# Turning ten of eighteen normalised tiles by DMA through DRAM instead of on TensorE

## The chip, the cores and the metric

The kernel runs on one core of a Trainium2 chip. The metric is the device time of one execution in microseconds (us), from the first to the last instruction with what lies around it. Below, PE is TensorE (PEld its weight loads), DVE is VectorE, ACT is ScalarE, POOL is GpSimd and SP is SyncE, whose queue issues every DMA of this kernel.

## What is computed

Sliding-window attention, cut here to what matters, then a feed-forward block with a softmax-weighted activation and a LayerNorm (FFN 1), then a gated feed-forward block (FFN 2), all in float32:

```python
scores = where(mask, scale * q @ k.T + bias, -1e9)      # 4 x 8 heads, 576 tokens, window 128
x = (softmax(scores) @ v)                               # 2304 tokens x 512

h = x @ w_in                                            # 2304 x 1024
solu = h * softmax(h)
ln = (solu - mean(solu)) / sqrt(var(solu) + 1e-6) * g_ln
y = ln @ w_out                                          # 2304 x 512

g = y @ w_gate                                          # 2304 x 1536
out = (g * sigmoid(g) * (y @ w_val)) @ w_out2           # 2304 x 512
```

## The kernel before

The 2304 tokens are 18 tiles of 128. The attention runs in 20 steps (4 batches of 5 query tiles) of four units of two heads. A unit's scores (line 441) are exponentiated (480), scaled by the inverse of the row sum (491 to 493, mostly on POOL), turned by PE with an identity matrix (511, "the probabilities' turns") and multiplied with v and with the difference vd of two v tiles (553). vd is made by POOL (403) from two loaded v tiles, of which three are kept.

FFN 1 takes a tile through three coroutines. `up(i)` multiplies x by w_in (24 products, line 639, "U" below), takes maximum, exponential, sums and variance (662 to 690), and normalises e, a tile of 128 tokens x 1024 features, in place on DVE or POOL (698). `flip(i)` turns e so that features lie on partitions: eight 128x128 transposes on PE into two PSUM banks (719), then ACT rounds the bank to the high part lnT0 (255), and DVE subtracts to get the low part lnT1 (259). Every product with FFN weights is made of three products of such high and low parts. `down1(i)` multiplies lnT by w_out (24 products, line 639, "the down product"), separates the result into its 16-bit halves (751) and stores these to DRAM (yscr), from where FFN 2 reads them back with six transposing DMAs (918).

FFN 2 follows when the attention is over: its first weights (dw<-w) are loaded then, and its products (968, 1130) fill the rest of the program.

The order of the work is made when the program is built. Coroutines hand operations to an `Emitter`, a list scheduler with a price for each operation and a rank for each coroutine (`i + LEAD` and offsets such as `O_FLIP`). It takes the operation that can start first by its prices, then the lowest rank. An operation with several possible engines (`high`, `low`) goes to the one that would end first, with a handicap `B_DVE` or `B_ACT` for DVE and ACT. `PATIENCE` says how long tiled products of the attention may be held back in favour of full-size ones. At run time each engine, and SP's DMA queue too, works through its list strictly in order and waits on semaphores. Four e tiles (`E1`) and two lnT pairs exist.

Of the kernel before, what the change touches and what calls it, by code (L numbers as in the profile page):

```python
# [11 lines left out]
U16 = mybir.dt.uint16  # L12
# [6 lines left out]
B, H, S, D = 4, 8, 576, 64  # L19
# [4 lines left out]
P = 128  # L24
NPAIR = H // 2
NQT = 5
NTT = NT // P
# [13 lines left out]
PXB = 2  # L41
EB = 5
Q = 32
PTB = 4
WHOLE = 20
VDB = 3
# [1 line left out]
LEAD = 3.373  # L48
R_FLIP = 0.751
R_DOWN = 3.0  # L50
PW_IN = [-0.63, -0.23, -0.29, -0.28, 0.25, 0.26, 0.43, 0.28]
PW_OUT = 5.23
B_DVE = 1802.444
B_ACT = 700.0
HALVES = [(0, 1), (1, 0), (0, 0)]
HB = NC2 // 2
# [10 lines left out]
O_FLIP = -1.299  # L67
O_LN = -0.416
O_SET = 0.102
O_FREE = -1.226  # L70


TOGETHER = 100000.0
PATIENCE = 540.469
LEAST = 3
BIAS = {"DVE": B_DVE, "ACT": B_ACT}

# [148 lines left out]
def attention_then_two_ffns(ctx: ExitStack, tc: tile.TileContext, qk, v, w_in, w_out, g_ln, w2, ident_d, base_d, tri_d, out):  # L226


    nc = tc.nc
    em = Emitter()  # L230
    PE, DVE, ACT, POOL, DMA = "PE", "DVE", "ACT", "POOL+", "DMA"
    DVEP, NONE = "DVE+", "POOL"
    yscr = nc.dram_tensor("yscr", [NT, 2, DM], U16).ap()
    ascr = nc.dram_tensor("ascr", [P, NC2, NT], F32).ap()
    wscr = nc.dram_tensor("wscr", [P, HB, 7 * 256], F32).ap()

    def t_act(n, sbuf=True, table=False):
        return (94 if sbuf else 51) + 94 * table + 0.833 * n

    def t_dve(n, fast=False):  # L240
        return 68 + (0.52 if fast else 1.042) * n

    def t_pool(n):
        return 149 + 2.104 * n

    def dma(dst, src, nbytes, deps=()):
        return (DMA, max(445.0, nbytes / 345.0), lambda: nc.sync.dma_start(dst, src), deps, 2000.0)

    const = ctx.enter_context(tc.tile_pool(name="const", bufs=1))
    ident = const.tile([P, P], F32, name="ident")  # L250
# [3 lines left out]
    def high(hi, src, n, sbuf=True):  # L254
        return [(ACT, t_act(n, sbuf), lambda: nc.scalar.copy(hi, src)),  # L255
                (DVEP if sbuf else DVE, t_dve(n, sbuf), lambda: nc.vector.tensor_copy(hi, src))]

    def low(lo, src, hi, n, sbuf=True):
        ways = [(DVEP if sbuf else DVE, t_dve(n), lambda: nc.vector.tensor_sub(lo, src, hi.bitcast(F32)))]  # L259
        if sbuf:  # L260
            ways.append((POOL, t_pool(n), lambda: nc.gpsimd.tensor_sub(lo, src, hi.bitcast(F32))))
        return ways
# [60 lines left out]
    at = esa.enter_context(tc.tile_pool(name="at", bufs=1, side="right"))  # L323
# [84 lines left out]

    e_s, pt_s, st_s, px_s = Slots(EB), Slots(PTB), Slots(EB), Slots(PXB)
    px_of, pts = {}, {}  # L410
# [4 lines left out]
    def score(c, qd):  # L415
# [19 lines left out]
        def scores():  # L435
            for j in range(2):
                for i in range(0, n, Q):
                    o, k0, w = (j * 256, 0, P) if t == 0 else (j * 256 + i, (t - 1) * P + i, P + Q)
                    for r in range(2):
                        rows = slice(r * D, (r + 1) * D)  # L440
                        nc.tensor.matmul(banks[ks[r]][i:i + Q, o:o + w], raw[c][rows, 2 * qd + j, i:i + Q],  # L441
                                         kt[rows, 2 * qd + j, k0:k0 + w], start=True, stop=True)
# [12 lines left out]
    def attend(u):  # L455
# [50 lines left out]
        tp = banks[k][:, 0:2 * P].rearrange("p (j q) -> p j q", j=2)  # L506
        pt = at.tile([P, 2, 2, P], F32, tag="pt", bufs=PTB, name="pt")

# [93 lines left out]
    def load_in():  # L602
        for half in range(2):
            cs = slice(half * 512, half * 512 + 512)
            for r in range(KM):
                def one(half=half, r=r, cs=cs):
                    yield from decode(win[0][:, r, cs], win[1][:, r, cs], w_in[r * P:(r + 1) * P, cs])
                d = em.start(one(), PW_IN[half * KM + r])
                chain(d, win_ok[half][r])
# [16 lines left out]

    lnT, es = {}, {}
    h_s, e1_s, ln_s, ys_s = Slots(HU), Slots(E1), Slots(2), Slots(1)
    upped = [Done() for _ in range(NTT)]
    normed = [Done() for _ in range(NTT)]  # L630
    flipped = [[Done(), Done()] for _ in range(NTT)]
# [72 lines left out]

    def flip(i):
        yield normed[i]
        if i:
            yield flipped[i - 1][1]
        yield ln_s
        lnT[i] = [m1.tile([P, KF1, P], F32R, tag=f"lnT{a}", bufs=2, name=f"lnT{a}") for a in range(2)]  # L710
        e = es[i]
        tail_ = []
        for q in range(2):
            bk = yield bank_s
            tp = banks[bk].rearrange("p (k c) -> p k c", k=4)

            def turn(q=q, tp=tp):
                for k in range(4):
                    nc.tensor.transpose(tp[:, k], e[:, q, k * P:(k + 1) * P], ident)

            hi, lo = (y[:, 4 * q:4 * q + 4] for y in lnT[i])
            x = yield (PE, 436, turn, (), 0.0, O_FLIP)
            y = yield (high(hi, tp, 512, False), [x], 0.0, O_LN)
            y = yield (low(lo, tp, hi, 512, False), [y], 0.0, O_LN)
            em.give(bank_s, y, bk)
            tail_.append(y)
        em.give(e1_s, x)
        for q, y in enumerate(tail_):
            yield y
            flipped[i][q].settle(y.time)  # L730
# [452 lines left out]
    for bank in banks:  # L1183
        halves = bank.rearrange("p (j c) -> p j c", j=2)
        nc.vector.memset(halves[:, :, P + Q:2 * P], 0.0)
        nc.vector.memset(halves[:, :, 0:P - Q], 0.0)
    for c in range(NS):
# [55 lines left out]
```

## Time and profile before

| | us |
|---|---|
| median of 3 runs | 755.77 |
| lowest, highest | 754.22, 757.95 |
| the profiled execution | 753.33 |
| its span | 751.5 |
| PE busy in the span | 717.4 (95%) |
| DVE, ACT, POOL busy | 554.5, 458.2, 225.4 |

The span runs from the first to the last instruction of the core; 1.83 us of the execution lie around it. Busy times count what an engine executes; instructions on PE overlap, so their durations don't add up to time. Idle time of an engine costs nothing by itself unless the engine sets the pace. Rows of the profile are in a section of their own below. A row of instructions in time gives start, length, engine, line, operation, output and inputs with their shapes and count, and in brackets the idle time of the engine ahead of it and what ended that.

### The profile page before, as it was taken

The page shows a single profiled execution, that of the slowest core. Times are in us where ns is not written, and L with a number is a line of the kernel's source. Part 1 is how long each engine was busy: PE and PEld are TensorE (multiplying, and loading weights), DVE is VectorE, ACT ScalarE, POOL GpSimd, SP SyncE. Part 2 cuts the span into 40 slices and gives each one's busy share as a digit, 9 for nine tenths or more (in the row PEclk, how much of TensorE's full clock was granted, in tenths as well). Part 3 has the DMA queues.
Part 4 walks back from the last instruction along what each step waited for, and adds up shares of the span by engine and source line. Part 5 has one row for each costly group of instructions (what it writes and reads, how often), then busy time and mean ns, then how long its engine had stood idle before and what let it go on. Part 6 is the DMA issues. An engine that isn't in the chain of part 4 may idle for free. (4 is left out here: it accounts for less than half of the span.)

```text
span 751.5 us, 14447 instructions
## 1 busy us (share of the span) xinstructions
PE 717.4 (95%) x5164; PEld 637.3 (85%) x5164; DVE 554.5 (74%) x1522; ACT 458.2 (61%) x1129; POOL 225.4 (30%) x240
## 2 busy tenths in 40 slices
PE   3879989999999999999999999999999999999997
PEld 1547667778788887888899999999899999999997
DVE  4788985676657665989879766876664599887965
ACT  7899996666656665687466555655553575442531
POOL 3686673333332422550024331221310000220200
PEclk9999999999999999999999999999999999999999
DMA  8753221222221006153755545554341698786951
GB/s 267 220 190 107 85 73 49 92 72 64 72 65 29 22 15 157 54 155 94 179 186 159 185 137 175 176 167 157 119 147 64 240 351 289 255 290 210 304 161 64
DMA packets 68328, 110.84 MB, mean 147 GB/s; under 512 B 24992, under 2 KB 37664, under 8 KB 68256
## 3 DMA queue, kind: packets, MB, share of 16 engines
q1 hardware_dynamic: 68256, 109.93, 44.9%
q8 instruction: 40, 0.66, 0.3%
q14 instruction: 32, 0.26, 0.1%
HBM read 76.09 MB, written 29.10 MB: 140 GB/s over the span
## 5 line engine op out<-in xcount | busy, mean ns | idle before, releaser
L968 PE MATMUL bank<-yt,w 128*128 128x384 f32 x1008 | 183.3, 337 | 2.6 <-ACT t L989 1.6
L968 PEld LDWEIGHTS bank<-yt,w 128*128 128x128 f32 x1008 | 175.5, 188 | 5.6 <-ACT set L989 2.6
L1130 PE MATMUL bank<-w,wo 128*128 128x384 f32 x756 | 132.8, 336 | 0.0
L1130 PEld LDWEIGHTS bank<-w,wo 128*128 128x128 f32 x756 | 132.4, 188 | 0.0
L301 POOL TENSOR_TENSOR db<-db,dw 128x512 int32<-128x512 int32 x52 | 72.1, 1387 | 187.6 <-DVE db L299 140.1
L639 PE MATMUL bank<-wout,lnT 128*128 128x512 f32 x432 | 102.8, 392 | 0.1
L968 PE MATMUL bank<-shared,w 128*128 128x384 f32 x504 | 96.5, 340 | 2.2 <-ACT set L991 1.4
L639 PEld LDWEIGHTS bank<-wout,lnT 128*128 128x128 f32 x432 | 80.3, 188 | 17.5 <-issue 0.8
L968 PEld LDWEIGHTS bank<-shared,w 128*128 128x128 f32 x504 | 87.3, 188 | 7.0 <-ACT set L989 2.3
L480 ACT ACTIVATE e<-e,st 128x128 f32<-128x128 f32 (+1 forms) x160 | 62.6, 402 | 35.8 <-DVE st L475 33.6
L639 PE MATMUL bank<-shared,shared 128*128 128x512 f32 x288 | 81.9, 416 | 1.1 <-ACT shared L255 1.1
L493 POOL TENSOR_TENSOR e<-e,st 128x256 f32<-128x256 f32 (+1 forms) x68 | 42.1, 622 | 77.7 <-DVE st L486 68.2
L639 PEld LDWEIGHTS bank<-shared,shared 128*128 128x128 f32 x288 | 52.3, 194 | 13.4 <-issue 2.0
L255 ACT CAST w<-t 128x768 fp32r<-128x768 f32 (+2 forms) x33 | 26.4, 809 | 42.2 <-DVE t L1084 29.5
L293 ACT ACTIVATE dw<-dw 128x512 int32<-128x512 uint32 x52 | 35.2, 676 | 14.0 <-DMA dw<-w 9.9
L475 DVE CUSTOM_DVE_ANT_0 e<-bank,bias 128x128 f32<-128x128 f32 (+1 forms) x160 | 38.3, 282 | 4.6 <-PE bank L441 2.4
L994 DVE TENSOR_TENSOR set<-set,bank 128x384 f32<-128x384 f32 x34 | 18.8, 553 | 30.4 <-PE bank L968 23.3
L441 PE MATMUL bank<-keys,raw 64*32 64x160 f32 (+1 forms) x1152 | 31.8, 322 | 9.7 <-DMA keys<-qk 7.7
L511 PE MATMUL bank<-ident,e 128*128 128x128 f32 (+1 forms) x160 | 29.8, 291 | 10.8 <-POOL e L493 4.3
L639 PE MATMUL bank<-shared 128*128 128x512 f32 x144 | 38.9, 391 | 0.0
L511 PEld LDWEIGHTS bank<-ident,e 128*128 128x128 f32 (+1 forms) x160 | 18.7, 146 | 23.5 <-POOL e L493 7.9
L255 ACT CAST w<-db 128x512 fp32r<-128x512 f32 (+1 forms) x47 | 26.8, 570 | 19.0 <-POOL db L301 14.5
(106 smaller groups left out, 1221.7 us busy)
## 6 DMA issues: line engine op xcount, KB each, us to landing
dw<-w SPq DMA_DIRECT2D x36, 512.0 KB, 3.9
t<-ascr SPq DMA_DIRECT2D x21, 768.0 KB, 5.7
ascr<-set SPq DMA_DIRECT2D x34, 384.0 KB, 2.7
later<-ascr SPq DMA_DIRECT2D x15, 768.0 KB, 5.5
wo<-wscr SPq DMA_DIRECT2D x6, 896.0 KB, 7.4
raw<-qk SPq DMA_DIRECT2D x19, 256.0 KB, 2.9
yscr<-ys SPq DMA_DIRECT2D x18, 256.0 KB, 2.0
wscr<-db SPq DMA_DIRECT2D x18, 256.0 KB, 4.3
```

Of the source, the lines that this page charges most:

```text
L255: return [(ACT, t_act(n, sbuf), lambda: nc.scalar.copy(hi, src)), (DVEP if sbuf else DVE, t_dve(n, sbuf), lambda: nc.vector.tensor_copy(hi ...
L293: r = yield (ACT, t_act(512), lambda: nc.scalar.activation(a, lw, AF.Copy, scale=2.0 ** -29), (), 0.0, O_DEC)
L301: x = yield (POOL, t_pool(512), lambda: nc.gpsimd.tensor_tensor(b.bitcast(I32), b.bitcast(I32), a, ALU.add), [x, r], 0.0, O_DEC)
L441: nc.tensor.matmul(banks[ks[r]][i:i + Q, o:o + w], raw[c][rows, 2 * qd + j, i:i + Q], kt[rows, 2 * qd + j, k0:k0 + w], start=True, stop=True)
L475: d = yield (DVE, t_dve(P), lambda j=j: nc.vector.tensor_tensor_reduce(e[0:n, j], sc[0:n, j * 256:j * 256 + P], bias[0:n, 2 * pr + j, bs], ...
L480: ex.append((yield (ACT, 93 + t_act(P, True, True), lambda j=j: nc.scalar.activation(e[0:n, j], e[0:n, j], AF.Exp, bias=st[0:n, j:j + 1], ...
L493: eng.tensor_tensor(e[0:n], e[0:n], st[0:n, 6:8].unsqueeze(2).to_broadcast([n, 2, P]), ALU.mult)
L511: nc.tensor.transpose(tp[:, j, 0:n], e[0:n, j], ident[0:n, 0:n])
L639: nc.tensor.matmul(o, terms[m][0], terms[m][1], start=(m == 0), stop=(m == len(terms) - 1))
L968: nc.tensor.matmul(o, l, r, start=first and m == 0, stop=m == 5, skip_group_check=True)
L994: g2 = yield (DVE, t_dve(NH), lambda: nc.vector.tensor_add(t[:, 1], t[:, 1], sb), [x3, u2], 0.0, O_FREE)
L1130: nc.tensor.matmul(o, w[:, b], ob[k, i][a][:, j], start=i == 0 and m == 0, stop=i == HB - 1 and m == 2)
```

## The change

For tiles 4 to 13 `flip(i)` no longer uses PE. Each half q of e (512 features) is copied into a tile pl with the two 16-bit halves of each word in two planes (on ACT, DVE or POOL; `halves_of`). pl is stored to DRAM (lscr, 256 KB), and a transposing DMA reads it back into the same half of e, now with features on partitions. The high and low parts of lnT are then made from e in SBUF, the high part by ACT or DVE, the low part by DVE or POOL. e is given back only after that. Two pl tiles exist. The other eight tiles are turned by PE as before. Four numbers of the scheduler change as well. (escr is declared and not used.)

```diff
+FLIP_BY_DMA = range(4, 14)
+PLB = 2
...
-PW_IN = [-0.63, -0.23, -0.29, -0.28, 0.25, 0.26, 0.43, 0.28]
+PW_IN = [-0.63, -0.23, -0.29, -0.28, 0.25, 0.17, 0.43, 0.28]
-B_DVE = 1802.444
+B_DVE = 1863.684
...
-O_FREE = -1.226
-TOGETHER = 100000.0
-PATIENCE = 540.469
+O_FREE = -1.17
+TOGETHER = 96722.643
+PATIENCE = 36.086
...
+    lscr = nc.dram_tensor("lscr", [NTT, 2, P, 2, 512], U16).ap()
...
+    def turn_by_dma(dst, src, nbytes, deps=()):
+        return (DMA, max(445.0, nbytes / 250.0), lambda: nc.sync.dma_start_transpose(dst, src), deps, 2200.0)
+
+    def halves_of(dst, src, n):
+        words = src.bitcast(U16).rearrange("p (c h) -> p h c", h=2)
+        return [(ACT, t_act(2 * n), lambda: nc.scalar.copy(dst, words)),
+                (DVEP, t_dve(2 * n), lambda: nc.vector.tensor_copy(dst, words)),
+                (POOL, t_pool(2 * n), lambda: nc.gpsimd.tensor_copy(dst, words))]
...
     def flip(i):
         yield normed[i]
+        e = es[i]
+        if i in FLIP_BY_DMA:
+            r = e.rearrange("p q (k t) -> p q k t", k=4)
+            words = r.rearrange("p q k t -> p q (k t)").bitcast(U16).rearrange("p q (k t) -> p q k t", k=4)
+            back = []
+            for q in range(2):
+                yield pl_s
+                pl = at.tile([P, 2, 512], U16, tag="pl", bufs=PLB, name="pl")
+                x = yield (halves_of(pl, e[:, q], 512), (), 0.0, O_FLIP)
+                x = yield dma(lscr[i, q], pl, 262144, [x])
+                em.give(pl_s, x)
+                x = yield turn_by_dma(words[:, q], lscr[i, q].rearrange("t h c -> (t h) c"), 262144, [x])
+                back.append(x)
+            yield back[0]
         if i:
             yield flipped[i - 1][1]
         yield ln_s
         lnT[i] = [m1.tile([P, KF1, P], F32R, tag=f"lnT{a}", bufs=2, name=f"lnT{a}") for a in range(2)]
-        e = es[i]
+        if i in FLIP_BY_DMA:
+            ends = []
+            for q in range(2):
+                hi, lo = (y[:, 4 * q:4 * q + 4] for y in lnT[i])
+                y = yield (high(hi, r[:, q], 512), [back[q]], 0.0, O_LN)
+                y = yield (low(lo, r[:, q], hi, 512), [y], 0.0, O_LN)
+                ends.append(y)
...
+            em.give(e1_s, y)
+            return
```

New lines are numbered higher than old ones: products of FFN 1 stand at 653 (639), the probabilities' turns at 524 (511), the turns of normalised tiles at 758 (719), loads and stores at 251 (247).

Since the scheduler sets the order, the change moves instructions well beyond the turns. The first place is PE around the first down product. Before, with bank_84 the up product of a half tile, wout and lnT_915 the first down product, e the probabilities, and e_1015 the normalised tile 2:

```order
L639 MATMUL bank_84<-shared_74,shared_73 128x512 x4
L639 MATMUL bank_84<-shared_73,shared_74 128x512 x4
L639 MATMUL bank_84<-shared_73 128x512 x4
L639 MATMUL bank_80<-wout_76,lnT_915 128x512 x8
L639 MATMUL bank_80<-wout_75,lnT_916 128x512 x8
L639 MATMUL bank_80<-wout_75,lnT_915 128x512 x8
L511 MATMUL bank_83<-ident,e 128x128 x2
L719 MATMUL bank_86<-ident,e_1015 128x128 x4
```

The same place on PE in the changed kernel:

```order
L653 MATMUL bank_84<-shared_74,shared_73 128x512 x4
L653 MATMUL bank_84<-shared_73,shared_74 128x512 x2
L524 MATMUL bank_85<-ident,e 128x128 x2
L653 MATMUL bank_83<-wout_76,lnT_915 128x512 x8
L653 MATMUL bank_83<-wout_75,lnT_916 128x512 x8
L653 MATMUL bank_83<-wout_75,lnT_915 128x512 x8
L524 MATMUL bank_81<-ident,e 128x128 x2
L524 MATMUL bank_82<-ident,e 128x128 x2
L653 MATMUL bank_84<-shared_73,shared_74 128x512 x2
L653 MATMUL bank_84<-shared_73 128x512 x4
```

Six of the twelve up products moved behind the first down product, and a pair of the probabilities' turns moved ahead of it.

The second place is POOL ahead of that down product: the last two rows of w_out (wout1), e1 a normalised tile, e the probabilities, mst the statistics of a tile. Before:

```order
L261 TENSOR_TENSOR wout1_76<-db_1298,wout0_75 128x512
L695 TENSOR_TENSOR mst_1150<-mst_1150,mhalf_59 128x1
L261 TENSOR_TENSOR wout1_76<-db_1365,wout0_75 128x512
L698 TENSOR_SCALAR e1_1278<-e1_1278,mst_1150 128x512 x2
L493 TENSOR_TENSOR e_1438<-e_1438,st_1439 128x256
```

Now:

```order
L274 TENSOR_TENSOR wout1_76<-db_1298,wout0_75 128x512
L709 TENSOR_TENSOR mst_1150<-mst_1150,mhalf_59 128x1
L506 TENSOR_TENSOR e_1436<-e_1436,st_1437 128x256
L274 TENSOR_TENSOR wout1_76<-db_1365,wout0_75 128x512
L712 TENSOR_SCALAR e1_1278<-e1_1278,mst_1150 128x512 x2
L506 TENSOR_TENSOR e_1522<-e_1522,st_1523 128x256
L260 COPY pl_1579<-e1_1278 128x1024
```

A scaling of probabilities (e_1436, which ACT did before) stands ahead of the last row of w_out, and the first separation into 16-bit planes follows.

The third place is POOL in the second half of the attention. Before, with e1_2451 the normalised tile 8, e1_2640 tile 9, and e the probabilities:

```order
L698 TENSOR_SCALAR e1_2451<-e1_2451,mst_2213 128x512 x2
L493 TENSOR_TENSOR e_2556<-e_2556,st_2557 64x256
L493 TENSOR_TENSOR e_2558<-e_2558,st_2559 64x256
L493 TENSOR_TENSOR e_2568<-e_2568,st_2569 64x256
L493 TENSOR_TENSOR e_2570<-e_2570,st_2571 64x256
L695 TENSOR_TENSOR mst_2450<-mst_2450,mhalf_59 128x1
L698 TENSOR_SCALAR e1_2640<-e1_2640,mst_2450 128x512 x2
```

Now, with e1_2444 tile 8 and e1_2634 tile 9:

```order
L712 TENSOR_SCALAR e1_2444<-e1_2444,mst_2190 128x512 x2
L260 COPY pl_2568<-e1_2444 128x1024
L506 TENSOR_TENSOR e_2562<-e_2562,st_2563 64x256
L506 TENSOR_TENSOR e_2564<-e_2564,st_2565 64x256
L506 TENSOR_TENSOR e_2577<-e_2577,st_2578 64x256
L506 TENSOR_TENSOR e_2579<-e_2579,st_2580 64x256
L709 TENSOR_TENSOR mst_2443<-mst_2443,mhalf_59 128x1
L274 TENSOR_TENSOR lnT1_2685<-e1_2444,lnT0_2684 128x512 x2
L712 TENSOR_SCALAR e1_2634<-e1_2634,mst_2443 128x512 x2
L260 COPY pl_2775<-e1_2634 128x1024
```

Tile 8's separation and, once it is back from DRAM, its two subtractions stand between the scalings of probabilities, and the subtractions stand ahead of tile 9's normalisation. SP's queue there has two stores and two transposing reads per tile among the attention's loads. On the whole PE has 80 turns fewer, DVE 20 subtractions to lnT1 fewer; POOL has 20 such subtractions and 8 separations more, ACT 12 separations more, and SP 40 DMAs more.

## Rows read from the trace of the kernel before

**Rows 1.** Busy time by stretch: us, then PE, PEld, DVE, ACT, POOL, clock, DMA.
```profile
110.00:340.00 230.00, 229.25 (x1908) 184.99 (x1908) 159.47 (x610) 150.49 (x448) 85.85 (x110) 1.00 0.24 73
340.00:560.00 220.00, 215.22 (x1200) 207.53 (x1199) 168.84 (x313) 129.05 (x255) 53.38 (x45) 1.00 0.50 159
...
140.00:280.00 140.00, 139.40 (x1392) 112.00 (x1391) 95.30 (x428) 89.58 (x302) 50.43 (x71) 1.00 0.17 52
```

**Rows 2.** PE in time, at the turns of tiles 6, 10 and 13.
```profile
171.15 1.04 PE L719 MATMUL bank<-ident,e 128*128 128x128 f32 x8
172.02 0.82 PE L511 MATMUL bank<-ident,e 128*128 128x128 f32 x6
...
234.62 1.36 PE L719 MATMUL bank<-ident,e 128*128 128x128 f32 x8
235.82 0.82 PE L511 MATMUL bank<-ident,e 128*128 128x128 f32 x6
...
283.68 1.09 PE L719 MATMUL bank<-ident,e 128*128 128x128 f32 x8
284.71 0.58 PE L511 MATMUL bank<-ident,e 64*128 64x64 f32 x6
```

**Rows 3.** PE's weight loads in time, at changes of form.
```profile
167.05 0.20 PEld L553 LDWEIGHTS bank<-pt,vd 128*64 128x64 f32 x4 [0.35 <-issue]
...
168.08 2.59 PEld L639 LDWEIGHTS bank<-wout,lnT 128*128 128x128 f32 x12 [0.17 <-issue]
```

**Rows 4.** Groups of instructions: count, busy us, mean ns, idle; the last from 140 to 280 us.
```profile
L259 DVE TENSOR_TENSOR lnT<-bank,lnT 128x512 fp32r<-128x512 f32 x36 | 23.9, 684 | 8.4 <-ACT lnT L255 8.2
L751 ACT COPY ys<-bank 128x1024 uint16<-128x1024 uint16 x18 | 18.1, 1005 | 8.1 <-PE bank L639 7.3 <-ACT w L255 0.9
L261 POOL TENSOR_TENSOR shared<-db,shared 128x512 fp32r<-128x512 f32 x8 | 10.1, 1272 | 2.4 <-ACT shared L255 2.4
...
L698 POOL TENSOR_SCALAR e<-e,mst 128x512 f32<-128x512 f32 x16 | 12.2, 776 | 0.8
```

**Rows 5.** PE and POOL in time, at the first down product.
```profile
109.72 2.11 PE L639 MATMUL bank<-shared,shared 128*128 128x512 f32 x8
110.98 1.30 POOL L261 TENSOR_TENSOR wout<-db,wout 128x512 fp32r<-128x512 f32 x1 [0.40 <-ACT wout L255]
112.57 5.61 PE L639 MATMUL bank<-wout,lnT 128*128 128x512 f32 x24
```

**Rows 6.** POOL and PE in time: tile 9's normalisation, turns and down product.
```profile
204.54 1.53 POOL L698 TENSOR_SCALAR e<-e,mst 128x512 f32<-128x512 f32 x2
...
212.97 0.62 POOL L493 TENSOR_TENSOR e<-e,st 128x256 f32<-128x256 f32 x1 [0.24 <-DVE st L486]
...
219.27 1.04 PE L719 MATMUL bank<-ident,e 128*128 128x128 f32 x8
...
245.51 5.61 PE L639 MATMUL bank<-wout,lnT 128*128 128x512 f32 x24
```

**Rows 7.** DMA issues (count, KB, median us to landing); line 918 on SP's queue (ns).
```profile
t<-ascr SPq DMA_DIRECT2D x21, 768.0 KB, 5.7
yscr<-ys SPq DMA_DIRECT2D x18, 256.0 KB, 2.0
...
L918 SPq DMA_TRANSPOSE t<-yscr x6: 3054/3274/4268, 287.7 to 358.8; - x6
DMA to landing us min/median/max: 5.2/5.8/7.8
```

**Rows 8.** POOL and DVE in time, at FFN 2's inputs.
```profile
299.68 3.00 POOL L698 TENSOR_SCALAR e<-e,mst 128x512 f32<-128x512 f32 x2
...
300.50 0.95 DVE L259 TENSOR_TENSOR yt<-t,yt 128x768 fp32r<-128x768 f32 x1
```

**Rows 9.** POOL and PE in time, from v's difference to the first product with it.
```profile
214.06 2.54 POOL L403 TENSOR_TENSOR vd<-v 128x512 f32<-128x512 f32 x2 [0.47 <-DMA v<-v]
...
237.95 0.44 PE L553 MATMUL bank<-pt,vd 128*64 128x128 f32 x4
```

More of the change, by code (lines that the diff above doesn't have):

```diff
@@ L233, in attention_then_two_ffns @@
     yscr = nc.dram_tensor("yscr", [NT, 2, DM], U16).ap()
+    escr = nc.dram_tensor("escr", [H // 2 * B * NQT, P, 2, 2 * P], U16).ap()
+    lscr = nc.dram_tensor("lscr", [NTT, 2, P, 2, 512], U16).ap()
     ascr = nc.dram_tensor("ascr", [P, NC2, NT], F32).ap()
@@ L628, in attention_then_two_ffns @@
     h_s, e1_s, ln_s, ys_s = Slots(HU), Slots(E1), Slots(2), Slots(1)
+    pl_s = Slots(PLB)
     upped = [Done() for _ in range(NTT)]
@@ L710, in flip @@
         lnT[i] = [m1.tile([P, KF1, P], F32R, tag=f"lnT{a}", bufs=2, name=f"lnT{a}") for a in range(2)]
-        e = es[i]
+        if i in FLIP_BY_DMA:
[5 more added lines that the diff above has]
+                ends.append(y)
+            for q, y in enumerate(ends):
+                yield y
+                flipped[i][q].settle(y.time)
+            em.give(e1_s, y)
+            return
         tail_ = []
```

## The prediction

> **What bounds the kernel now.** I read the table of stretches first [rows 1], then PE's own order in time [rows 2, 5, 6]. In the stretch from 110 to 340 us, where the attention steps, both products of FFN 1 and the turns share PE, PE is busy for 229.25 of 230 us at a granted clock of 1.00; between 140 and 280 us it is busy for 139.40 of 140, while DVE has 95.30, ACT 89.58 and POOL 50.43. PE thus idles 0.75 us in 230. So in the stretch that the change touches the bound is PE's own sequence: an instruction that leaves PE shortens the program by what it held there, as long as nothing else comes to end later than PE.
>
> **What the change takes from PE.** Each of the ten tiles loses eight 128x128 turns. They overlap, so what counts is start to start and not how long one lasts. Tile 6 starts its eight at 171.15, and the next instruction starts at 172.02: 0.87 us. Tile 13, whose next turns are 64 wide, has 283.68 to 284.71: 1.03 us. Of the ten tiles six are like the first (0.87 to 0.88), three like the second (1.02 to 1.03), and tile 10 has 234.62 to 235.82, 1.20 us, which I count at 0.87, because the rest looks like a wait inside it [rows 2]. Sum: 7 x 0.87 + 3 x 1.03 = 9.2 us. Bounds: 10 x 0.87 = 8.7, and 6 x 0.87 + 3 x 1.03 + 1.20 = 9.5.
>
> On PE one turn of a row thus takes 0.87 / 8 = 0.109 us [rows 2]. The Trainium skill's page "VectorE: DVE Perf Modes", section The three transpose paths, gives 390 ns for a 128x128 transpose on TensorE and 1309 ns by DMA, and its rules say TensorE where PSUM will do; by its figure for TensorE the ten tiles would save 80 x 0.39 = 31 us, an estimate that the trace contradicts.
>
> **What it adds on the path: a gap at the first down product.** PE is also re-ordered. Before, twelve products of an up stage (the U that starts at 109.72) stand ahead of the first down product, which starts at 112.57, right when POOL has finished the last row of w_out (110.98 + 1.30 = 112.28) [rows 5]. Now only six products and one pair of turns stand there, and POOL has one more scaling of probabilities ahead of that last row. In the old trace POOL idles 0.40 us in this place [rows 5]; such a scaling takes 0.62 [rows 6], so w_out would be there some 0.2 us later, at about 112.5. The down product starts when it did, but less is done by then: six products are half of 109.72 to 112.57, about 1.4 us, and a pair of turns gives back 0.2 (two of 0.109). I take 1.3 us, with what the scaling adds; ends 0 (if w_out comes earlier in the new order) and 2.0 (if the scaled probabilities come later too).
>
> **Changes of PE's form.** Between full-size products and the tiled ones of the attention PE's weight loads idle 0.17 to 0.35 us [rows 3]. The new order has 115 runs of one form on PE, the old one 112: 3 x 0.26 = 0.8 us; ends 0 and 1.1.
>
> **What it adds beside the path.** Per tile, by the nearest rows [rows 4]:
> - Two separations into 16-bit planes (1024 elements). Twelve of twenty stand on ACT, where the copy of ys, the same size and type from PSUM, takes 1.005 us. Eight stand on POOL, where no such copy is shown; a one-input operation of half the size takes 0.776 us, a two-input one 1.272, so 1.6 to 2.5; I take 1.6, since a copy has one input. Per tile on average: 1.2 on ACT, 0.8 x 1.6 = 1.3 on POOL.
> - The two roundings to hi stay on ACT. The two subtractions to lo move from DVE (684 ns each) to POOL (1.272 each): DVE -1.4, POOL +2.5.
> - Two stores of 256 KB and two transposing reads. A store of this size lands in 2.0 us. The six transposes in the trace are three times as large: 3.27 us of SP's queue each, and 5.8 to landing [rows 7]. No engine waits for SP itself; what is queued behind on it are loads of v, raw and k, which are asked for well ahead (the difference of two v tiles made at 214.06 serves a product at 237.95 [rows 9]). By size the new ones hold SP for 1.1 us; as long as the old ones is the other end.
>
> A tile comes every 16.1 us (171.15 to 283.68 is seven tiles [rows 2]). Of these ACT works 89.58 / 140 x 16.1 = 10.3, then 11.5; DVE 11.0, then 9.6; POOL 5.8, then 9.6; the new cadence would be about 15.2. No engine comes near PE. The length of the way doesn't show either: tile 9 is normalised at 204.54 + 1.53 = 206.07, turned by PE from 219.27 on, and first used by its down product at 245.51 [rows 6]. The new way (separation 1.0 to 2.5, store 2.0, two issues 2.2, landing at most 5.8, two subtractions 2.5) takes 13.5 to 15 us, inside the 39; even the old instant of the turn is missed by no more than 2 us, so the four e tiles and the two lnT pairs come free in time. From FFN 2 on SP's order is the same as before, and PE's too; the first FFN 2 weights are fetched after the last attention step, so FFN 2 starts earlier by what is saved. I put what is beside the path at 0 and the risk into the rivals.
>
> **Sum.** -9.2 + 1.3 + 0.8 = -7.1 us against the profiled execution's 753.33 (span 751.5): 746.2. The median of the runs shown is 2.44 above that, and the prediction is for the median: 755.77 - 7.1 = 748.7. With the ends of the terms: -9.5 + 0 + 0 gives 746.3, and -8.7 + 2.0 + 1.1 gives 750.2.
>
> **Rivals.**
> 1. POOL's longer queue makes the attention late, and part of the gain is lost. On POOL the probabilities are scaled among the new work. In the old trace the last scaling of a step ends at 212.97 + 0.62 = 213.59, and PE comes to the probabilities' turns around 219.27: over 5 us of cover [rows 6]. The new 4 to 5 us of a tile with a copy, all ahead of it, would just fit. But two normalisations that take 1.53 us at 204.54 take 3.00 at 299.68, while DVE works on FFN 2's inputs from SBUF [rows 6, 8]; at twice the time 8 to 10 us stand ahead, and PE waits 3 to 5 us in such a tile. It costs from a slowing of 1.2 on. One tile of ten so: 752 to 754. For: POOL waits in order for each transposing read before its subtraction. Against: from 140 to 280 us POOL's sixteen normalisations have a mean of 776 ns [rows 4], nothing is slowed there. The Trainium skill (SBUF — State Buffer, Who interferes with whom) says that a DVE operation with two SBUF inputs and a GpSimd one that reads SBUF block each other; the pair at 299.68 and 300.50 agrees with it.
> 2. The transposing reads make it slower, by way of POOL's list. From tile 8 on a tile's subtractions stand on POOL ahead of the next tile's separation, so that POOL can't begin a tile before the one ahead is back: normalisation 1.53 [rows 6], separation 1.6, store 2.0 to landing, issue 1.1, landing L, rounding about 0.7, subtractions 2.5 [rows 4, 7] make a loop of 9.4 + L. L lies between 2.0 and 5.8: the plain loads of 768 KB land in 5.7, the transposing ones in 5.8, so by these rows a transposing one of 256 KB is about as quick as a plain one, 2.0. The loop is 11.4 to 15.2 then, inside the cadence. If a third of the size takes as long as the slowest of the six did (7.8 to landing, and 3.27 on SP for the one ahead), with the dearer separation of 2.5, it is 1.5 + 2.5 + 2.0 + 3.3 + 7.8 + 0.7 + 2.5 = 20.3 us; then POOL paces six tiles at 20.3 instead of 16.1, +25 us. Tiles 4 to 7 still save 3.6, and the 2.1 of the order are lost: 755.8 + 25 - 3.6 + 2.1 = 779. It decides from a loop of 17.0 on (6 x 0.9 + 2.1 - 3.6 = +3.9). For: no row shows a transposing read of this size. Against: the six of the trace. By the figure of 1309 ns on the Trainium skill's page "VectorE: DVE Perf Modes" (The three transpose paths) a tile's sixteen 16-bit blocks would take 20.9 us, an estimate, more than the cadence; the trace disagrees, since 768 KB, 24 such blocks, land in 5.8 us [rows 7].
> 3. Nothing to be seen: the time saved is waited for again after the border to FFN 2, where PE has 4.8 us of gaps between 340 and 560 us [rows 1]. About 755.5. Against: that work starts from the end of the attention and moves with it.
>
> **Chances.** Forecast 0.71 (746.3 to 751); rival 1 0.14; rival 3 0.06; rival 2 0.05; better than the terms 0.04. I predict 748.7. The range runs from 745.8 to 753.5; it leaves out most of the better end, rivals 2 and 3 and a little of rival 1. A measurement of this kernel tells some 0.5%, 3.8 us, from no change, so faster means below 752.0: the forecast, the better end and a third of rival 1, 0.80. Same, up to 759.5: the rest of rival 1 and rival 3, 0.15. Slower: 0.05.
>
> **What the profile after would show.** If right: 64 turns of normalised tiles on PE instead of 144; PE busy for about 708 us, with gaps from 140 to 280 us as small as now; a gap of about 1.3 us ahead of the first down product; a cadence near 15.2 us; POOL busy 38 to 46 us longer; transposing reads of e that hold SP for about 1.1 us. Rival 1: PE waits for POOL's scaled e ahead of the probabilities' turns. Rival 2: POOL's subtractions wait for transposing reads, for several us in each tile, and PE for POOL. Rival 3: PE's gaps after 320 us grow by as much as was saved. The step that takes PE's sequence for the bound would be wrong if PE shows new waits of several us for lnT between 120 and 290 us.

## The result, and the profile after

| | before | after |
|---|---|---|
| median, us | 755.17 (4 runs) | 746.72 (4 runs) |
| lowest to highest | 754.22 to 757.95 | 744.56 to 748.00 |
| the profiled execution, its span | 753.33, 751.5 | 744.56, 742.8 |
| PE, POOL busy | 717.4, 225.4 | 708.3, 257.0 |

The ratio is 0.988 (95% interval 0.984 to 0.992): 8.4 us faster. Measured once more, beside later runs, it was 0.991 (0.989 to 0.993), 6.8 us. The forecast was 7.1 us and 748.7.

The stretches of the changed kernel, columns as in [rows 1]:

```profile
110.00:340.00 230.00, 226.24 (x1856) 180.97 (x1857) 154.56 (x597) 168.17 (x472) 119.06 (x138) 1.00 0.46 122
340.00:560.00 220.00, 217.54 (x1219) 210.62 (x1218) 167.67 (x311) 127.65 (x253) 53.66 (x45) 1.00 0.48 157
140.00:280.00 140.00, 138.84 (x1378) 109.20 (x1377) 90.37 (x427) 105.67 (x331) 78.68 (x96) 1.00 0.43 114
```

From 140 to 280 us PE idles 1.2 of 140 us, 0.6 before. POOL went from 50 to 79, ACT from 90 to 106, and the share of the DMA engines from 0.17 to 0.43, and PE goes on nearly without a gap. Its waits from 105 to 292 us, all that are listed (us, times, longest):

```profile
PE bank L524 <- POOL e L506: 0.5, 1, 0.5
PE bank L653 <- ACT shared L268: 0.5, 1, 0.5
PE bank L566 <- ACT pt L534: 0.4, 1, 0.4
```

None of them is for lnT. The first down product, with PE and then POOL in time, to be read against [rows 5]:

```profile
110.34 1.66 PE L653 MATMUL bank<-shared,shared 128*128 128x512 f32 x6 [0.53 <-ACT shared L268]
111.84 0.38 PE L524 MATMUL bank<-ident,e 128*128 128x128 f32 x2
112.25 5.72 PE L653 MATMUL bank<-wout,lnT 128*128 128x512 f32 x24
...
110.56 0.62 POOL L506 TENSOR_TENSOR e<-e,st 128x256 f32<-128x256 f32 x1
111.14 1.29 POOL L274 TENSOR_TENSOR wout<-db,wout 128x512 fp32r<-128x512 f32 x1
```

The scaling stands ahead of w_out's last row, which ends at 112.43 (112.28 before), and the down product starts at 112.25 (112.57) with six products ahead of it instead of twelve. So it starts 0.18 us before that row is ready: it didn't wait for it. The two kernels are still together at the scores ahead of these products (PE at line 441, now 454). PE and ACT there, before and now:

```profile
109.01 0.77 PE L441 MATMUL bank<-keys,raw 64*32 64x160 f32 x32
109.13 0.37 ACT L255 CAST shared<-bank 128x256 fp32r<-128x256 f32 x1 [0.22 <-PE bank L553]
...
109.04 0.77 PE L454 MATMUL bank<-keys,raw 64*32 64x160 f32 x32
109.32 0.71 ACT L323 ACTIVATE db<-db,gln 128x512 f32<-128x512 f32 x1
109.93 0.36 ACT L268 CAST shared<-bank 128x256 fp32r<-128x256 f32 x1
```

ACT now decodes a weight before it rounds the attention's output (shared), and PE waits 0.53 us for the rounding ahead of its six products; before, these products started at 109.72 [rows 5]. The new work by groups (count, busy, mean ns, idle):

```profile
L274 POOL TENSOR_TENSOR lnT<-e,lnT 128x512 fp32r<-128x512 f32 x20 | 25.3, 1283 | 4.9 <-ACT lnT L268 4.8
L258 ACT COPY pl<-e 128x1024 uint16<-128x1024 uint16 x12 | 12.6, 1056 | 1.5 <-POOL e L712 1.5
L260 POOL COPY pl<-e 128x1024 uint16<-128x1024 uint16 x8 | 8.3, 1038 | 0.4
```

The transposing reads as one line of the code on SP's queue (ns, lowest/median/highest), and their landing:

```profile
L254 SPq DMA_TRANSPOSE e<-lscr x20: 1226/1249/1979, 118.0 to 270.9; - x20
DMA to landing us min/median/max: 3.0/3.6/5.0
```

The span by three landmarks: the first down product starts 0.32 us earlier (112.25), the last product with v stands at 281.60 instead of 289.52, so that the stretch between is 7.60 shorter, and from there to the end it is 461.20 instead of 461.98, 0.78 shorter.

### The profile page after: what moved, and what is told of

Its sections match the earlier page's. It is cut to its first block, busy times and chain, and to the rows that moved or that the text cites. A ratio compares the mean times of both kernels' runs of the same rounds, so it can differ in the third digit from the quotient of the medians.

```text
span 742.8 us, 14409 instructions
## 1 busy us (share of the span) xinstructions
PE 708.3 (95%) x5084; PEld 627.8 (85%) x5084; DVE 544.5 (73%) x1499; ACT 469.9 (63%) x1146; POOL 257.0 (35%) x268
```

## The experiments

Medians in us, each with its own runs of the kernel before; D0 is the start of the first down product, V the start of the last product with v, F the time from V to the first product of line 1130 (1169 in the changed kernel), all from the profiled execution. From V to that product all these kernels have the same 1713 matmuls on PE, in the same order.

| kernel | median | before | ratio (95%) | D0 | V | F |
|---|---|---|---|---|---|---|
| before | 755.17 | | | 112.57 | 289.52 | 318.4 |
| the change | 746.72 | 755.17 | 0.988 (0.984 to 0.992) | 112.25 | 281.60 | 317.9 |
| the change again | 746.21 | 753.03 | 0.991 (0.989 to 0.993) | 111.90 | 281.49 | 319.1 |
| numbers alone | 755.65 | 752.81 | 1.004 (1.002 to 1.006) | 112.63 | 292.04 | 318.3 |
| turning alone | 746.48 | 752.81 | 0.991 (0.990 to 0.993) | 113.25 | 283.38 | 318.4 |
| turns left out | 748.94 | 752.81 | 0.995 (0.994 to 0.996) | 112.95 | 287.08 | 317.3 |
| turns and parts left out | 749.30 | 754.25 | 0.993 (0.992 to 0.994) | 114.02 | 285.75 | 318.4 |
| way left out | 746.56 | 752.81 | 0.991 (0.989 to 0.993) | 111.66 | 281.25 | 320.0 |
| read twice | 785.21 | 754.25 | 1.040 (1.038 to 1.043) | 112.52 | 316.76 | 325.3 |
| second half read twice | 749.84 | 753.03 | 0.996 (0.994 to 0.998) | 112.72 | 286.05 | 318.2 |
| separations on POOL | 751.25 | 754.25 | 0.996 (0.995 to 0.997) | 111.99 | 283.50 | 321.3 |
| five tiles | 752.14 | 754.25 | 0.997 (0.996 to 0.999) | 112.88 | 286.39 | 322.3 |
| twelve tiles | 751.22 | 753.03 | 0.998 (0.996 to 0.999) | 116.16 | 288.16 | 317.7 |
| fourteen tiles | 754.02 | 753.03 | 1.002 (1.001 to 1.003) | 132.64 | 294.08 | 318.4 |

F scatters from 317.3 to 322.3 without the run that reads twice. Some of that is TensorE's clock: in the profiles of the change again, the way left out and the separations on POOL PE idles 2.6 to 2.8 us for ACT near 340 us, and behind that the granted clock is 0.50 for some 3.4 us. From 341.1 to 344.5 us the change again gets 13 products done, the first profile of the change 22 at a clock of 1.00. D0 scatters too: up to there eight of these runs have the change's sequence on PE, its own two among them, and their D0 lies between 111.66 and 112.88; four have that of the kernel before, from 112.57 to 114.02. A difference in one profile of a few us behind V, or of one us in D0, is therefore no evidence for an edit. The stretch from D0 to V is: 176.95 us before, 169.35 and 169.59 in the two profiles of the change.

**The change again.**

> The changed kernel once more, beside the runs that follow. Its first measurement had a ratio of 0.9879 (0.9844 to 0.9915). Forecast as recorded: -7.1 us. The terms as the traces have them (attention ends 7.9 earlier; the stretch behind it varies by 1 to 5 us between kernels with the same instructions): ratio 0.9885 to 0.9905, -7 to -8.5 us.

It gave 6.8 us, with V within 0.11 of the first profile.

**The numbers alone and the turning alone.** The first has

```diff
-FLIP_BY_DMA = range(4, 14)
+FLIP_BY_DMA = range(0)
```

> The four scheduler numbers of the change, and no tile turned by DMA: PE keeps its 144 turns. In this order six up products stand behind the first down product, as in the changed kernel, and PE has 111 runs of one form (112 before). By the terms of the forecast: 1.3 for the gap at the first down product, less 1 x 0.26 for one change of form, together +1.0 us, 756.2 against 755.2. Rival: the surplus of the change over the forecast (8.4 instead of 7.1) comes from the new numbers, and the order alone makes the kernel faster by 1 to 2 us, 754 or lower.

It came out 2.8 us slower, not 1.0. V is 2.5 later, and D0 stands where it was. Half of that is the six products missing ahead of D0, less the pair of turns. The rest are waits that the order of the kernel before didn't have; the largest of PE's waits from 105 to 292 us in the run with the numbers alone:

```profile
PE bank L524 <- ACT ys L790: 0.8, 1, 0.8
PE bank L758 <- DVE st L498: 0.8, 1, 0.8
PE bank L653 <- ACT shared L268: 0.5, 1, 0.5
```

The second keeps FLIP_BY_DMA and puts the old four numbers back:

```diff
-B_DVE = 1863.684
+B_DVE = 1802.444
...
-PATIENCE = 36.086
+PATIENCE = 540.469
```

> Tiles 4 to 13 turned by DMA with the scheduler numbers of the kernel before. Here twelve up products stand ahead of the first down product, as before, so that the gap of 1.3 is gone, but PE has 120 runs of one form, 8 more than before: 8 x 0.26 = 2.1 us. By the terms of the forecast -9.2 + 0 + 2.1 = -7.1 us, 748.1 against 755.2. Rival: a change of form costs PE nothing here, since weight loads run ahead; then -9.2, 746.0, faster than the change as made.

It gained 6.3 us (5.6 to 7.6 by the interval). The rival of free changes of form (9.2) falls. From D0 to V it takes 0.8 us longer than the change, though 1.2 us of products less are left to do there; of these 2.0 some 0.4 are listed waits more, and five more runs of a form at 0.26 would make 1.3, which fits; no run isolates it. With the turning, the new numbers bring nothing that can be measured (6.8 and 6.3); without it they cost 2.8.

**The turns left out** of the kernel before, in its own order, with nothing in their place.

```diff
                 for k in range(4):
-                    nc.tensor.transpose(tp[:, k], e[:, q, k * P:(k + 1) * P], ident)
+                    if not 4 <= i < 14:
+                        nc.tensor.transpose(tp[:, k], e[:, q, k * P:(k + 1) * P], ident)
```

> The kernel before in its own order, with the 80 turns of tiles 4 to 13 left out and nothing in their place: the parts of lnT of these tiles are made of whatever the bank holds, so the output is not the reference's. Forecast for the turns' price on PE, start to start: -9.2 us (bounds 8.7 and 9.5), 746.0 against 755.2. Rival: the turns cost PE more than their own time, since each tile's turns also wait or delay what follows; then -10 to -11 us, 744 to 745, and the change has hidden costs of 2 us beside the path.

Both missed: 3.9 us. V moved by 2.4 only. From D0 to V PE is busy for 8.5 us less (167.73 instead of 176.20), but it idles 6.4 us instead of 0.75: two thirds of the turns' time came back as waits. PE and then ACT of this run in time, at the place where tile 9's turns were:

```profile
218.43 1.04 PE L511 MATMUL bank<-ident,e 128*128 128x128 f32 x8
219.22 1.62 PE L639 MATMUL bank<-shared,shared 128*128 128x512 f32 x6
221.19 0.66 PE L553 MATMUL bank<-pt,v 128*64 128x128 f32 x8 [0.35 <-DVE lnT L259]
...
218.63 1.01 ACT L752 COPY ys<-bank 128x1024 uint16<-128x1024 uint16 x1 [0.28 <-PE bank L639]
219.53 0.38 ACT L521 COPY pt<-bank 128x256 f32<-128x256 f32 x1
219.80 0.61 ACT L255 CAST lnT<-bank 128x512 fp32r<-128x512 f32 x1
220.28 0.95 ACT L521 COPY pt<-bank 128x256 f32<-128x256 f32 x3
```

After the down product ACT copies ys, then the turned probabilities with a rounding between them, and is done at about 221.2; PE has only the probabilities' turns and six products for this time, and then waits for the copies (the name in the bracket is the last event seen, the product needs pt, which ACT had just copied). In the kernel before the eight turns of the tile stood there as well [rows 6], 0.87 us, and covered this. So here a turn was not only work: 0.35 us of the 0.87 lay beside work of ACT that takes its time anyway. The other large waits of this run, 0.5 to 1.0 us each, are put down to ACT, DVE and POOL.

**Turns and parts left out.** To see whether the roundings in that chain are the whole cause, they and the subtractions are left out too:

```diff
+            idle = lambda ways: [(w[0], w[1], lambda: None) for w in ways] if 4 <= i < 14 else ways
-            y = yield (high(hi, tp, 512, False), [x], 0.0, O_LN)
-            y = yield (low(lo, tp, hi, 512, False), [y], 0.0, O_LN)
+            y = yield (idle(high(hi, tp, 512, False)), [x], 0.0, O_LN)
+            y = yield (idle(low(lo, tp, hi, 512, False)), [y], 0.0, O_LN)
```

> As the run with the turns left out, in the order of the kernel before, but for tiles 4 to 13 the roundings to lnT0 (ACT) and the subtractions to lnT1 (DVE) are left out too; their down products read the lnT of tile 3. With the turns alone left out the kernel gained 3.9 us, not 9.2, and PE waited 0.35 to 0.69 us in a tile ahead of the products with the probabilities, while ACT worked through the copy of ys, the copies of the probabilities and the two roundings between them (2.8 us against 2.4 of PE work). Theory: the turns on PE were the cover of this ACT work; without the roundings (0.6 each) ACT's chain is shorter than PE's 2.4, and the whole price of the turns shows: -8.5 to -9.2 us, 743.6 to 744.3 against 752.8. Rival: the wait is for something else (the probabilities' scaling, banks), and the gain stays at 4 to 5 us, 748 to 749.

5.0 us: the theory as put falls, the roundings are only a part. From 140 to 280 us, the run with the turns left out (columns as in [rows 1]):

```profile
140.00:280.00 140.00, 134.41 (x1333) 106.13 (x1334) 96.61 (x431) 90.02 (x304) 50.28 (x71) 1.00 0.16 52
```

The same stretch of this run:

```profile
140.00:280.00 140.00, 136.57 (x1351) 107.88 (x1350) 87.09 (x420) 83.40 (x291) 50.23 (x71) 1.00 0.17 53
```

PE idles 5.6 and then still 3.4 us of 140, where the kernel before has 0.6 [rows 1]. The waits that stay (0.3 to 0.7 us each) stand at the probabilities' turns, behind ACT's copy of ys, POOL and DVE, and one at their products. Several chains beside PE thus ended within a few tenths of PE. Of all 9.2 us of turns the old order could give back 4 to 5 (from D0 to V 2.8 and 5.2).

The changed kernel gives back more; its order is made for the shorter PE sequence. A like place in it, behind tile 8's down product, PE and then ACT:

```profile
229.81 1.04 PE L524 MATMUL bank<-ident,e 128*128 128x128 f32 x8
230.60 1.62 PE L653 MATMUL bank<-shared,shared 128*128 128x512 f32 x6
232.66 0.44 PE L566 MATMUL bank<-pt,vd 128*64 128x128 f32 x4 [0.43 <-ACT pt L534]
...
230.75 0.60 ACT L268 CAST lnT<-e 128x512 fp32r<-128x512 f32 x1
231.52 1.36 ACT L534 COPY pt<-bank 128x256 f32<-128x256 f32 x4 [0.16 <-DVE pt L531]
232.78 0.62 ACT L268 CAST lnT<-e 128x512 fp32r<-128x512 f32 x1
233.30 1.01 ACT L790 COPY ys<-bank 128x1024 uint16<-128x1024 uint16 x1
```

The copy of ys and one rounding now stand behind the probabilities' copies. PE still waits 0.43 us here, but this is the only tile with such a wait.

**The way left out.** Is anything beside the path paid for? The changed kernel without its separations, stores and transposing reads:

```diff
-                x = yield dma(lscr[i, q], pl, 262144, [x])
+                x = yield (DMA, 262144 / 345.0, lambda: None, [x], 2000.0)
...
-                x = yield turn_by_dma(words[:, q], lscr[i, q].rearrange("t h c -> (t h) c"), 262144, [x])
+                x = yield (DMA, 262144 / 250.0, lambda: None, [x], 2200.0)
```

> The changed kernel in its own order, with separations, stores and transposing reads of tiles 4 to 13 left out (20 copies and 40 DMAs; the roundings and subtractions stay and read e as it is, so the output is not the reference's). Forecast: all of this lies beside PE's sequence and costs nothing, so 746.7, as the changed kernel, to within 1 us. Rival: the queue of SP, the traffic or the copies on ACT and POOL still cost something, and the kernel without them is faster by 2 us or more, 744.7 or lower.

Ratio 0.991, the same as the change again, and V is at 281.25 (281.49). 20 copies and 40 DMAs cost nothing, to within the 0.2% of either interval. This run also sets the two orders beside each other. Neither it nor the run with the turns left out has turns or a way for tiles 4 to 13; from D0 to V PE idles 6.4 us in the old order, 1.3 in the new one, in which the subtractions stand on POOL as well.

**How thin is the cover?** The transposing read of a half, issued twice, first for both halves and then for the second half only; as the order is made, nothing else moves.

```diff
+        def twice():
+            nc.sync.dma_start_transpose(dst, src)
+            return nc.sync.dma_start_transpose(dst, src)
-        return (DMA, max(445.0, nbytes / 250.0), lambda: nc.sync.dma_start_transpose(dst, src), deps, 2200.0)
+        return (DMA, max(445.0, nbytes / 250.0), twice, deps, 2200.0)
```

> The changed kernel with each transposing read issued twice, one behind the other into the same half of e, in the same order otherwise. The second waits for the first, so that each tile's way is longer by two landings and two issues, 2 x (1.25 + 2.4 to 3.6) = 7 to 10 us. Forecast as recorded (the way of 13.5 to 15 us lies inside 39): no change against the changed kernel, ratio 0.988 to before. Rival 2 as recorded (POOL can't begin a tile before the one ahead is back; with the measured copy of 1.04 and landing of 3.6 the loop is 12.4 us, and decides from 17.0 on): the loop becomes 19.5 to 22.5, six tiles are paced at 4 to 7 us more than the cadence of 15.4, and the kernel is 24 to 42 us slower than the changed one, 768 to 786 against a kernel before of 752.8.

31 us slower than before, some 37 slower than the change (1.040 against 0.991). The number is rival 2's, the place for the most part is not. The largest of ACT's waits from 112 to 320 us (us, times, longest):

```profile
ACT lnT L271 <- DMA e<-lscr: 20.6, 9, 4.0
```

ACT and then PE in time at one tile of this run:

```profile
217.68 0.62 ACT L271 CAST lnT<-e 128x512 fp32r<-128x512 f32 x1 [2.99 <-DMA e<-lscr]
222.02 0.62 ACT L271 CAST lnT<-e 128x512 fp32r<-128x512 f32 x1 [3.72 <-DMA e<-lscr]
222.54 0.76 ACT L537 COPY pt<-bank 128x128 f32<-128x128 f32 x4
...
223.19 0.69 PE L569 MATMUL bank<-pt,vd 64*64 64x64 f32 x8 [6.75 <-ACT pt L537]
```

The stretch behind it:

```profile
223.00:229.00 6.00, 5.81 (x99) 4.69 (x100) 2.15 (x18) 3.79 (x11) 3.51 (x4) 0.50 0.42 114
```

ACT waits for the reads with its two roundings, in order; the probabilities' copies are queued behind, and PE waits for these. After that pause PE works at a granted clock of 0.50 for some 6 us (1.00 from 200 to 216), which makes the wait dearer. From D0 to V this kernel takes 34.9 us longer than the change: PE idles 23.6 us more, and the other 11 us are slower work, at a mean granted clock of 0.92 over the stretch. Nor do all waits run through the probabilities' copies. Of PE's 24.6 us of listed waits 10.3 are for these, 5.4 for POOL's scaled probabilities, and 8.9 for ACT's copy of ys, which once waited 8.7 us for a store that stood on SP's queue behind the doubled reads. The smaller dose was to tell POOL's loop from this:

> The changed kernel with only the second half's transposing read issued twice (the first run of this kind repeated both halves and was 39 us slower than the change). A tile's way is longer by one issue and landing, 3.6 us. Theory from that run: what breaks is not POOL's list but ACT's: the rounding to lnT0 waits there for the read, with the copies of the turned probabilities behind it, and PE waits for those. In the changed kernel the second read of the tile issued at 196.22 lands some 0.3 to 0.8 us ahead of its rounding, the next (211.20) 1.7, the others 3.6 to 6. So one to two tiles come late by 2 to 3 us each: 3 to 5 us slower than the changed kernel. Rival (POOL's loop, 12.4 + 3.6 + 1.25 = 17.3 us against 17.0 from which it decides): the cadence goes from 15.4 to 17.3 in six tiles, 11 us slower. The recorded cover of 39 us less 15: no change.

3.6 us slower than the change, as the theory of ACT's queue has it; POOL's loop (11 us) and the cover of 39 (none) fall. ACT and PE in time in this run, at the tile named in the expectation:

```profile
204.62 0.62 ACT L272 CAST lnT<-e 128x512 fp32r<-128x512 f32 x1 [2.16 <-DMA e<-lscr]
205.14 0.76 ACT L538 COPY pt<-bank 128x128 f32<-128x128 f32 x4
...
205.78 0.45 PE L570 MATMUL bank<-pt,vd 64*64 64x64 f32 x8 [2.28 <-ACT pt L538]
```

The changed kernel at the same place:

```profile
201.39 1.13 ACT L268 CAST lnT<-e 128x512 fp32r<-128x512 f32 x2
202.42 0.74 ACT L534 COPY pt<-bank 128x128 f32<-128x128 f32 x4
...
203.05 0.45 PE L566 MATMUL bank<-pt,vd 64*64 64x64 f32 x8
```

One read more and ACT's second rounding is 2.16 us late, and PE 2.28. Only one other tile loses anything of size (0.42, as in the change itself). From D0 to V the run takes 4.0 us longer than the change; PE idles 2.5 of them and is busy 1.5 us longer with the same instructions; behind that wait the granted clock is 0.50 for 3.4 us:

```profile
206.70:210.10 3.40, 3.40 (x81) 2.78 (x70) 2.04 (x17) 1.78 (x6) 2.42 (x3) 0.50 0.35 106
```

**Separations on POOL**, those that stand on ACT, at the same place in the program.

```diff
-        return [(ACT, t_act(2 * n), lambda: nc.scalar.copy(dst, words)),
+        return [(ACT, t_act(2 * n), lambda: nc.gpsimd.tensor_copy(dst, words)),
```

> The changed kernel with the twelve separations that stand on ACT issued on POOL instead, at the same place in the program: POOL works 12 x 1.04 = 12.5 us more, at most 1.04 to 2.1 in a tile, ACT as much less. Forecast: POOL's scaled probabilities have about 5 us of cover, so nothing changes, within 1 us of the changed kernel, ratio 0.988 to before. Rival 1 as recorded (POOL's longer queue makes the attention late): PE waits for scaled probabilities in most of the ten tiles, 3 to 6 us lost, ratio 0.992 to 0.996.

0.996: rival 1, at its lower bound in size. PE in time, the two places where it waits for scaled probabilities:

```profile
154.59 0.44 PE L524 MATMUL bank<-ident,e 128*128 128x128 f32 x2 [0.51 <-POOL e L506]
175.97 1.01 PE L524 MATMUL bank<-ident,e 128*128 128x128 f32 x4 [1.93 <-POOL e L506]
```

The first is in the changed kernel too, the second is new. It is one place and not most of the ten tiles. V moves by 1.9 of the 3.8 us; what the rest is stays open, since it lies in F (the 3.4 us at the lower clock there are in the change again too).

**Other numbers of tiles**: range(4, 9), range(2, 14), range(0, 14).

```diff
-FLIP_BY_DMA = range(4, 14)
+FLIP_BY_DMA = range(4, 9)
```

> The changed kernel with five tiles (4 to 8) turned by DMA instead of ten. By the terms of the forecast: -5 x 0.87 for the turns, +1.3 for the gap at the first down product, +0.8 for 115 runs of a form = -2.3 us, 750.5 against 752.8. By the runs so far (the numbers alone +2.9, the change with ten tiles -8.4), if each tile is worth the same: half way, -2.8. Rival: a tile's gain is not its turns, since without them ACT's chain is late; the gain then depends on how well the order fits, and five tiles of an order made for ten give 0 to -1 us.

2.1 us, and V 3.1 earlier than before. The terms gave 2.3, which fits fixed costs of the order that are paid once and 0.87 for a tile. From D0 to V it gains 3.4, and the other five tiles of the change 4.2 more, 0.83 each; F is the longest of all here.

> The changed kernel with twelve tiles (2 to 13) turned by DMA. By the terms: turns -12 x 0.87 - 0.5 = -10.9; PE stands 12 up products further back at the first down product than in the kernel before, +2.9; 111 runs of a form, -0.3: -8.3 us to before, as the changed kernel or 0 to 1 us better. By the price per tile that the five and the ten tiles show (-2.1 and -8.4: 1.2 a tile): -10.8. Rival: the added separations fall in the time in which ACT decodes weights and w_out comes later; the first down product starts later than at 112.3, and the gain is 6 or less.

> The changed kernel with the first fourteen tiles (0 to 13) turned by DMA. By the terms: turns -14 x 0.87 - 0.5 = -12.7; 117 runs of a form, +1.3; work ahead of the first down product is done then and not lost: -11.4 us to before, if PE has work to do until tile 0 is back from DRAM. Rival: ACT is busy for 91 of the first 105 us, and the way of the first tiles can't be hidden there: the first down product comes some 5 us later than at 112.3 with PE idle ahead of it, and the gain is 4 to 6 us.

1.8 us faster and 1.0 slower: the rivals, with fourteen tiles beyond what was expected (D0 20 us later, not 5). The last row of w_out on POOL and the first down product on PE, with twelve tiles:

```profile
115.31 1.27 POOL L274 TENSOR_TENSOR wout<-db,wout 128x512 fp32r<-128x512 f32 x1 [2.02 <-ACT wout L268]
116.16 2.11 PE L653 MATMUL bank<-wout,lnT 128*128 128x512 f32 x8 [1.49 <-DVE shared L272]
```

The same with fourteen:

```profile
131.48 1.28 POOL L274 TENSOR_TENSOR wout<-db,wout 128x512 fp32r<-128x512 f32 x1 [2.31 <-ACT wout L268]
132.64 1.65 PE L653 MATMUL bank<-wout,lnT 128*128 128x512 f32 x6
```

POOL waits for ACT, and w_out is ready 4 and 20 us later than with ten. Yet in both the down product starts before its last row is ready (116.16 against 116.58, 132.64 against 132.76), so this row doesn't hold its start. With twelve, PE's wait of 1.49 us ends, by the bracket, with DVE's subtraction from the attention's output, which follows ACT's rounding. ACT has the separations and roundings of the first tiles in its list as well, which would make both late; it was not isolated. With twelve, D0 to V is also longer than with ten (172.00), and PE idles 4.0 us of it. None of the three beats the change.

## Why the prediction was right

By its own steps:

- **The bound.** Right for the changed kernel: PE idles 1.2 of 140 us, and leaving the whole way out gives nothing. PE is busy for 708.3 us (forecast 708), 64 turns remain, the cadence is 15.4 (240.30 to 255.76 and 271.12, the down products' starts; forecast 15.2).
- **-9.2 for the turns.** As a price it held only where the order was made anew. Between D0 and V the change gained 7.60, and the terms give 9.2 - 1.4 (the six products that moved there) + 0.2 - 0.8 = 7.2. In the old order the same 80 turns were worth 3.9. The step says "as long as nothing else comes to end later than PE"; I took that for granted from PE's busy share, without following the instruction behind the turns to what it waits for. At the tile shown ACT's chain to that instruction was 0.35 us too long without them, and from D0 to V 5.6 us of the 8.5 came back as waits.
- **+1.3 at the first down product.** The size was near, 0.9 in this pair of profiles (1.42 of products less a pair of turns of 0.22, less the start that is 0.32 earlier), with D0 scattering by over 1 us; the mechanism was wrong, and that the term fitted was luck. The step says that the product starts when POOL has finished the last row of w_out. In the changed kernel it starts 0.18 us before that; in the kernel before, the row was there 0.29 us ahead, and PE came from its twelve products without a listed wait. What PE loses there is above all the wait of 0.53 us for ACT's rounding of the attention's output. The runs with the new four numbers have it too (0.5 to 0.6 in those listed); the turning alone, with the old numbers, has not.
- **+0.8 for changes of form.** No run isolates it. The five tiles (2.1 against 2.3) and the turning alone (6.3 against 7.1) come within 0.8 us of the sums that contain it.
- **Nothing beside the path.** Right as a sum, by the way left out. The length of the way was added up without the rounding to hi (0.62). The separation on POOL was mis-sized: 1.04 us, not 1.6 to 2.5, and POOL's busy time grew by 31.6 instead of 38 to 46. The reads hold SP for 1.25 (1.1 by size) and land in 3.6, between the ends of 2.0 and 5.8. By the figure of 1309 ns on the Trainium skill's page "VectorE: DVE Perf Modes" (The three transpose paths) a read's eight blocks would take 10.5 us, an estimate that the 3.6 contradict.
- **The cover.** Wrong: "inside the 39". The 39 us ran from the normalisation to the down product, but what decides is the next instruction that waits for the read: ACT's rounding, with the probabilities' copies behind it. Its margin at one tile was under 1 us, and 3.6 us more of way cost 3.6 us. The prediction named who is queued behind POOL's subtraction, not who is behind ACT's rounding.
- **The rivals.** Rival 1 didn't come (0.5 us of PE's waits), and was nearer than its price says: 12 copies more on POOL cost 3.8 us (2.2 from D0 to V). Rival 2's limit exists, but mostly on ACT, and from a few us of delay, not from a loop of 17.0. Rival 3 is out: from V to the end the span is 0.78 shorter, and within the scatter of F.

## What to carry to other kernels

An instruction taken from the engine that sets the pace is worth its time only as far as what the engine meets next is ready earlier too: look up that next instruction's inputs and the queue in which they are made. When the order is made anew for the shorter sequence most of the price comes back, so ask for both. A transfer's cover ends at the first instruction that waits for it on an engine with an ordered queue, and what stands behind that instruction is late with it; the time to the last use says nothing.

## What the runs showed of the hardware

- The same copy of 1024 16-bit words from SBUF takes 1.04 us on POOL and 1.06 on ACT, while a rounding of 512 words takes 0.62 on ACT and a subtraction of 512 takes 1.28 on POOL.
- A transposing read of 256 KB lands in 3.6 us and holds SP's queue for 1.25, one of 768 KB takes 5.8 and 3.27 [rows 7]: three times the bytes, 1.6 times the landing.
- After PE had idled for 6.75 us its granted clock was 0.50 (the lower of its two levels, 1.2 GHz) from 223 to 229 us, and eight small products took 0.69 us instead of 0.45.
- With the same instructions on PE the time from V to line 1169's first product differed by up to 5 us between kernels (F); nearly all of PE's listed waits there are for ACT. In three profiles 3.4 us of it ran at a granted clock of 0.50 after PE had idled 2.6 to 2.8 us.
